# First-quad queries on a second DMA queue, last query rows moved out of the lead-in, idle transposes in their place, last token tile in two halves

## The chip, the cores and the metric

One core of a Trainium2 chip. The metric is the device time of one execution in microseconds (us). The kernels of one call ran on the same chip, with runs of the kernel before among them.

Names: TensorE is PE in the profile (PEld: its weight loads), VectorE DVE, ScalarE ACT, GpSimd POOL, SyncE SP; a trailing q (ACTq, SPq) is an engine's queue issuing transfers. The granted clock is the share of TensorE's full speed that the profile recorded; a dip is a stretch at 0.50, and a transpose is called cold when it ran at half clock. Fill is idle transposes put where TensorE would wait.

## The reference

Thresholded attention for 8 batches x 8 heads (576 rows of 64), then a gated two-matmul layer over the 4608 tokens:

```python
scores = scale * q @ k.T                       # scale = 1/8
thresh = max(scores, axis=-1) - tau
attn   = softmax(where(scores >= thresh, scores, -1e9))
x      = (attn @ v), heads side by side        # 4608 x 512
h      = x @ w_in                              # 512 x 2048
g      = h * clip(h + 3, 0, 6) / 6
out    = g @ w_out                             # 2048 x 512, float32
```

## The kernel before

The work of attention is cut into 144 slots, 9 for each quad (four heads). A slot computes scores for 128 query rows of two heads (TensorE), takes the row maximum while copying them out (VectorE), masks and exponentiates them (ScalarE) and normalizes them (GpSimd); from slot 22 on, matmuls of the gated layer fill the gaps. Before slot 0, keys and queries of the first quad must be loaded and transposed by TensorE: the lead-in. After slot 143 the rest of the gated layer runs: the tail.

```python
# loads of a quad, in this order, all on SyncE's queue: keys, queries, the last 64 rows of both, ...
def main(dst, src, h, order):
    nc.sync.dma_start(out=dst[:, :, h, :], in_=src[b, 4 * g + h, 0:512, :].rearrange(order, t=4))
...
def transpose_rest(quad):                      # last 64 rows of the four heads
    ps = bank("tr")                            # one PSUM bank
    nq, _, kr = nat[quad]
    nc.tensor.transpose(ps[:, 0:P], kr[:], identf[:])
    if by_pe(2 * quad):
        nc.tensor.transpose(ps[:, P:2 * P], nq[:, 1024:1152], identf[:])
    def evict():
        ...
        nc.vector.tensor_copy(out=qT[:, :, 512:S], in_=both[:, 1])     # query rows: used in slot 8 only
        copy_out(kT[0:64, :, S:S + 64], both[0:64, 0])                 # keys: used in slot 0
        copy_out(kT[64:P, :, 0:64], both[64:P, 0])
    return evict
...
warm_up(14)                                    # idle transposes, to raise the TensorE clock
...
evict = transpose_k(0)
warm_up(4)
evict_q = transpose_q(0)
evict()
evict_q()
transpose_rest(0)()
...
queue[0].tiles = scores(0, 0)
for n, sl in enumerate(queue):                 # the slots
    ...
    if n < 8:
        warm_up(6)
...
count = [0, 0]
def rest1(item, then):                         # tail: one gated item
    h = mm1(item, pool=ps_s if count[0] % 3 else None)     # ps_s: a pair of buffers, else a third one
    count[0] += 1
    mm1_gate(item, h, mm1_relu(h, on_act=True))
    ...
def rest2():                                   # tail: output tiles
    ...
        mm2_part(bb, mt, part, pool=ps_s if count[1] % 3 else None)
        if part == 3:
            flush()
            late.extend(mm2_out(bb, mt, on_act=(count[1] % 2 == 0)))
            count[1] += 1
```

## Time and profile before

| | kernel before |
|---|---|
| median of the first 3 runs | 561.12 us (561.0 to 562.59) |
| profiled execution | span 562.3 us, time 564.1 us, mean granted clock 0.989 |
| TensorE, ScalarE, VectorE busy | 95%, 84%, 75% |
| ScalarE's first activation (mask) of slots 0, 1, 2, 3 | 10.72, 13.59, 18.23, 21.31 us |
| last matmul to the end of the span | 558.25 to 562.3: 4.05 us |

A useful yardstick throughout is the start of each slot's first ScalarE activation (its mask). Slots follow each other in a fixed pattern, so two kernels' masks differ by a constant "lead" wherever nothing new happens; a step in the lead shows where time was won or lost. The lines themselves are shown with the prediction.

### The profile page before, as it was taken

The page shows a single profiled execution, that of the slowest core. Times are in us where ns is not written, and L with a number is a line of the kernel's source. Part 1 is how long each engine was busy: PE and PEld are TensorE (multiplying, and loading weights), DVE is VectorE, ACT ScalarE, POOL GpSimd, SP SyncE. Part 2 cuts the span into 40 slices and gives each one's busy share as a digit, 9 for nine tenths or more (in the row PEclk, how much of TensorE's full clock was granted, in tenths as well). Part 3 has the DMA queues.
Part 4 walks back from the last instruction along what each step waited for, and adds up shares of the span by engine and source line. Part 5 has one row for each costly group of instructions (what it writes and reads, how often), then busy time and mean ns, then how long its engine had stood idle before and what let it go on. Part 6 is the DMA issues. An engine that isn't in the chain of part 4 may idle for free.

```text
span 562.3 us, 11634 instructions
## 1 busy us (share of the span) xinstructions
PE 535.0 (95%) x3856; PEld 309.3 (55%) x3856; DVE 424.4 (75%) x1040; ACT 470.3 (84%) x999; POOL 305.2 (54%) x646
## 2 busy tenths in 40 slices
PE   7998798899999999999999999999999999999997
PEld 5665455455545565555555565655555565654663
DVE  3588787687878788787878798887978798883440
ACT  4799899798988999989898999899898999983540
POOL 1678878854556555655456555755556555561000
PEclk8899999899999999999999999999999999999999
DMA  5879999997689876978589867987699865453102
GB/s 110 135 110 166 162 160 184 207 148 144 112 159 153 151 153 127 208 139 155 114 150 170 159 137 146 174 160 146 127 137 175 167 124 117 101 109 86 38 20 75
DMA packets 286204, 77.52 MB, mean 138 GB/s; under 512 B 269248, under 2 KB 281536, under 8 KB 286144
## 3 DMA queue, kind: packets, MB, share of 16 engines
q1 hardware_dynamic: 268736, 67.86, 64.8%
q0 software_dynamic: 17408, 8.92, 13.7%
q8 instruction: 30, 0.49, 0.4%
q14 instruction: 30, 0.25, 0.2%
HBM read 36.70 MB, written 9.44 MB: 82 GB/s over the span
## 4 chain that ended last, share of the span: by engine, by line
PE 58%; DVE 11%; ACT 9%; issue 4%; POOL 1%; DMA 1%; SPq 1%; DVEq 0%; POOLq 0%
PE h L353 18%; PE o L382 17%; PE s L256 16%; DVE s L277 5%; ACT s L285 4%; PE av L323 3%; ACT s L290 3%; DVE g L370 2%; DVE r L364 2%; ACT r L362 2%; PE s L262 1%; PE tp L213 1%; PE ar L323 1%; DVE osb L390 1%; POOL pn L298 1%
## 5 line engine op out<-in xcount | busy, mean ns | idle before, releaser
L298 POOL TENSOR_SCALAR pn<-s,rinv 128x576 bf16<-128x576 f32 x288 | 211.6, 745 | 133.5 <-issue 58.5
L277 DVE TENSOR_SCALAR_CACHE_REDUCE s<-s 128x576 f32<-128x576 f32 x288 | 205.9, 752 | 44.9 <-PE s L256 35.2
L285 ACT ACTIVATE s<-s,bias 128x576 f32<-128x576 f32 x288 | 207.1, 766 | 36.8 <-POOL bias L280 35.7
L290 ACT ACTIVATE s<-s 128x576 f32<-128x576 f32 x288 | 192.7, 671 | 0.3
L256 PE MATMUL s<-kT,qT 64*128 64x288 f32 x1024 | 172.7, 435 | 5.4 <-DVE s L277 3.2
L353 PE MATMUL h<-xT,w_in_sb 128*128 128x320 bf16 (+1 forms) x1024 | 145.0, 287 | 5.5 <-DVE g L370 4.6
L382 PE MATMUL o<-w_out_sb,g 128*128 128x512 bf16 x576 | 140.9, 379 | 3.6 <-DVE osb L390 3.0
L353 PEld LDWEIGHTS <-w_in_sb 128*128 128x128 bf16 x1024 | 92.0, 97 | 68.4 <-issue 31.1
L256 PEld LDWEIGHTS s<-kT,qT 64*128 64x128 f32 x1024 | 94.8, 188 | 62.7 <-DVE s L277 24.9
L370 DVE SCALAR_TENSOR_TENSOR g<-r,h 128x512 bf16<-128x512 f32 (+1 forms) x128 | 96.4, 754 | 41.2 <-ACT r L362 39.3
L280 POOL TENSOR_SCALAR bias<-m 128x1 f32<-128x1 f32 x288 | 54.4, 189 | 69.0 <-DVE s L277 48.2
L382 PEld LDWEIGHTS <-g 128*128 128x128 bf16 x576 | 55.6, 98 | 58.2 <-issue 9.8
L362 ACT ACTIVATE r<-h,three 128x640 f32<-128x640 f32 (+1 forms) x74 | 54.4, 737 | 21.1 <-PE h L353 20.4
L290 ACT ACTIVATION_READ_ACCUMULATOR s<-s 128x1 f32 x288 | 54.2, 188 | 0.0
L364 DVE TENSOR_SCALAR r<-h 128x512 f32<-128x512 f32 (+1 forms) x54 | 40.5, 751 | 0.0
L390 DVE TENSOR_SCALAR osb<-o 128x512 f32<-128x512 f32 x31 | 21.0, 676 | 22.2 <-PE o L382 22.2
L323 PE MATMUL av<-pT,vm 128*64 128x512 bf16 x256 | 34.6, 392 | 2.0 <-ACT kT L203 2.0
L323 PEld LDWEIGHTS <-vm 128*64 128x64 bf16 x512 | 18.1, 111 | 25.2 <-issue 18.3
L293 DVE RECIPROCAL rinv<-rsum 128x2 f32<-128x2 f32 x144 | 23.0, 160 | 10.2 <-ACT s L290 9.5
L335 DVE CAST xT<-av 128x512 bf16<-128x512 f32 x32 | 21.8, 681 | 5.6 <-PE av L326 5.3
L277 DVE DVE_READ_ACCUMULATOR s<-s 128x1 f32 x288 | 23.9, 83 | 0.0
L388 ACT ACTIVATE osb<-o 128x512 f32<-128x512 f32 x5 | 3.0, 597 | 23.9 <-PE o L382 23.9
(42 smaller groups left out, 255.9 us busy)
## 6 DMA issues: line engine op xcount, KB each, us to landing
km<-in_k_dram SPq DMA_DIRECT2D x64, 128.0 KB, 3.0
out_dram<-osb SPq DMA_DIRECT2D x32, 256.0 KB, 2.4
nq<-in_q_dram SPq DMA_DIRECT2D x96, 72.0 KB, 2.7
vm<-in_v_dram POOLq DMA_DIRECT2D x16, 256.0 KB, 5.4
nq<-in_q_dram SPq DMA_DIRECT2D x16, 128.0 KB, 3.9
w_in_sb<-in_moe_w_in_dram POOLq DMA_DIRECT2D x16, 128.0 KB, 4.1
w_out_sb<-in_moe_w_out_dram POOLq DMA_DIRECT2D x16, 128.0 KB, 4.5
pT<-pn SPq DMA_TRANSPOSE x119, 3.4
```

Source lines behind the costliest of these rows:

```text
L256: nc.tensor.matmul(tiles[a][:, hf, 0:HALF], qT_of(pair)[a * 64:(a + 1) * 64, t * P:(t + 1) * P], keys(pair, a, hf), start=True, stop=True)
L277: nc.vector.tensor_scalar(out=sl.s[:, i, :].rearrange("p (a b) -> p a b", a=2), in0=ps[:, :, 0:HALF], scalar1=1.0, scalar2=None, op0=Alu.m ...
L280: nc.gpsimd.tensor_scalar(out=sl.bias[:, i:i + 1], in0=sl.m[:, i:i + 1], scalar1=-scale, scalar2=tau, op0=Alu.mult, op1=Alu.add)
L285: nc.scalar.activation(out=s, in_=s, func=Act.Prelu, bias=sl.bias[:, i:i + 1], scale=scale, alpha=REJECT)
L290: nc.scalar.activation(out=s, in_=s, func=Act.Exp, accum_out=sl.rsum[:, i:i + 1])
L298: nc.gpsimd.tensor_scalar(out=pn[:, i, :], in0=sl.s[:, i, :], scalar1=sl.rinv[:, i:i + 1], scalar2=1.0, op0=Alu.mult, op1=Alu.mult)
L323: nc.tensor.matmul(ps[a * 64:(a + 1) * 64, :], vm[:, 2 * hp + a, c * D:(c + 1) * D], pT[:, 5 * a + c, cols], start=(c == 0), stop=False)
L353: nc.tensor.matmul(hps[:, n, 0:w], w_in_sb[:, ki, (ni + n) * P:(ni + n + 1) * P], xT[b][:, ki, c0:c0 + w], start=(ki == 0), stop=(ki == KI ...
L362: nc.scalar.activation(out=r, in_=hps, func=Act.Relu, bias=three[:])
L364: nc.vector.tensor_scalar(out=r, in0=hps, scalar1=3.0, scalar2=0.0, op0=Alu.add, op1=Alu.max)
L370: nc.vector.scalar_tensor_tensor(out=gbuf[:, ni:ni + 2, c0:c0 + w], in0=r, scalar=6.0, in1=hps, op0=Alu.min, op1=Alu.mult)
L382: nc.tensor.matmul(o_ps[0], gbuf[:, ni, mt * P:(mt + 1) * P], w_out_sb[:, ni, :], start=(ni == 0), stop=(ni == NI - 1))
```

## The change

Four things: (1) the first queries are issued by ScalarE's queue, beside the keys on SyncE's; (2) the first quad's last query rows are transposed in slot 1; (3) six and eight idle transposes fill the places where TensorE waited; (4) in the tail the buffer rotation starts at 1, and the last token tile leaves in two halves, one by ScalarE and one by VectorE.

```diff
-        def main(dst, src, h, order):
-            nc.sync.dma_start(...)
+        def main(dst, src, h, order, by=nc.sync):
+            by.dma_start(...)
...
-                    main(..., q, 2 * n + a, "(t p) d -> p t d")
+                    main(..., q, 2 * n + a, "(t p) d -> p t d",
+                         by=nc.scalar if quad == n == 0 else nc.sync)
...
-    transpose_rest(0)()
+    transpose_rest(0, of_q=False)()
+    warm_up(6)
...
+        elif n == 1:
+            evict = transpose_rest(0, of_k=False)
...
+        if n == 0:
+            warm_up(8)
         if n + 1 < len(queue):
             queue[n + 1].tiles = scores(queue[n + 1].quad, queue[n + 1].slot)
...
-    count = [0, 0]
+    count = [1, 0]
+    def last_out():
+        ...
+        nc.scalar.activation(out=osb[:, 0:c], in_=o_ps[0][:, 0:c], func=Act.Copy, scale=1.0 / 6.0)
+        nc.scalar.dma_start(out=out[r0:r0 + P, 0:c], in_=osb[:, 0:c])
+        nc.vector.tensor_scalar_mul(out=osb[:, c:2 * c], in0=o_ps[0][:, c:2 * c], scalar1=1.0 / 6.0)
+        nc.sync.dma_start(out=out[r0:r0 + P, c:2 * c], in_=osb[:, c:2 * c])
```

More of the change, by code (lines that the diff above doesn't have):

```diff
@@ L85, in load_quad @@
         nq, km, kr = nat[quad]
-        def main(dst, src, h, order):
-            nc.sync.dma_start(out=dst[:, :, h, :], in_=src[b, 4 * g + h, 0:512, :].rearrange(order, t=4))
+        def main(dst, src, h, order, by=nc.sync):
+            by.dma_start(out=dst[:, :, h, :], in_=src[b, 4 * g + h, 0:512, :].rearrange(order, t=4))
         def blocks_q(n, a, j):
@@ L97, in load_q @@
                 for a in range(2):
-                    main(nq[:, 0:1024].rearrange("p (t h d) -> p t h d", h=4, t=4), q, 2 * n + a, "(t p) d -> p t d")
+                    main(nq[:, 0:1024].rearrange("p (t h d) -> p t h d", h=4, t=4), q, 2 * n + a, "(t p) d -> p t d",
+                         by=nc.scalar if quad == n == 0 else nc.sync)
             else:
@@ L226, in transpose_k, with transpose_rest @@
         return lambda: copy_out(kT_of(pair)[:, 64:576], ps[:])
-    def transpose_rest(quad):
+    def transpose_rest(quad, of_k=True, of_q=True):
         ps = bank("tr")
         nq, _, kr = nat[quad]
-        nc.tensor.transpose(ps[:, 0:P], kr[:], identf[:])
-        if by_pe(2 * quad):
+        of_q = of_q and by_pe(2 * quad)
+        if of_k:
+            nc.tensor.transpose(ps[:, 0:P], kr[:], identf[:])
+        if of_q:
             nc.tensor.transpose(ps[:, P:2 * P], nq[:, 1024:1152], identf[:])
@@ L237, in evict @@
             both = ps[:].rearrange("p (w n t) -> p w n t", n=2, t=64)
-            if by_pe(2 * quad):
+            if of_q:
                 nc.vector.tensor_copy(out=qT[:, :, 512:S], in_=both[:, 1])
-            copy_out(kT[0:64, :, S:S + 64], both[0:64, 0])
-            copy_out(kT[64:P, :, 0:64], both[64:P, 0])
+            if of_k:
+                copy_out(kT[0:64, :, S:S + 64], both[0:64, 0])
+                copy_out(kT[64:P, :, 0:64], both[64:P, 0])
         return evict
@@ L525 @@
     last = NQUAD - 1
-    count = [0, 0]
+    count = [1, 0]
+    def last_out():
+        osb = o_pool.tile([P, d_model], F32, tag="osb", name="osb")
+        r0, c = B * S - 64 - P, d_model // 2
+        nc.scalar.activation(out=osb[:, 0:c], in_=o_ps[0][:, 0:c], func=Act.Copy, scale=1.0 / 6.0)
+        nc.scalar.dma_start(out=out[r0:r0 + P, 0:c], in_=osb[:, 0:c])
+        nc.vector.tensor_scalar_mul(out=osb[:, c:2 * c], in0=o_ps[0][:, c:2 * c], scalar1=1.0 / 6.0)
+        nc.sync.dma_start(out=out[r0:r0 + P, c:2 * c], in_=osb[:, c:2 * c])
     def rest1(item, then):
@@ L539, in rest2 @@
                 flush()
-                late.extend(mm2_out(bb, mt, on_act=(count[1] % 2 == 0)))
+                if (bb, mt) == (B // 2 - 1, 8):
+                    last_out()
+                else:
+                    late.extend(mm2_out(bb, mt, on_act=(count[1] % 2 == 0)))
                 count[1] += 1
```

## The prediction

> **What bounds the kernel now.** I read the page first (clock row and chain), then the timeline of the first 24 us, one-microsecond windows of the clock there, and last the chain and timeline of the final 30 us, because the diff touches only the two ends. From the page:
>
> ```profile
> span 562.3 us, 11634 instructions
> PEclk8899999899999999999999999999999999999999
> PE 58%; DVE 11%; ACT 9%; issue 4%; POOL 1%; DMA 1%; SPq 1%; DVEq 0%; POOLq 0%
> ```
>
> TensorE carries most of the chain that ended last, ScalarE and VectorE most of the rest; DMA is 1%. The change leaves that middle alone. It can only move when the first softmax slot starts and how the end drains. The clock row shows its lowest digits (8) in the first two slices, which are the lead-in. The timeline of the lead-in (start, duration, engine, what, then idle time and its releaser):
>
> ```profile
> 1.37 3.06 PE L164 MATMUL warm<-identf 128*128 128x128 f32 x14 [1.37 <-POOL identf masks.py:199]
> ...
> 4.83 0.63 PE L213 MATMUL tp<-identf,km 128*128 128x128 f32 x4 [0.41 <-DMA km<-in_k_dram]
> ...
> 5.86 0.63 PE L213 MATMUL tp<-identf,nq 128*128 128x128 f32 x4
> ...
> 6.47 0.30 PE L231 MATMUL tr<-identf,kr 128*128 128x128 f32 x1
> 6.53 0.69 DVE L220 COPY qT<-tp 128x512 f32<-128x512 f32 x1 [4.95 <-PE tp L213]
> ...
> 7.59 0.30 PE L233 MATMUL tr<-identf,nq 128*128 128x128 f32 x1 [0.81 <-DMA nq<-in_q_dram]
> ...
> 7.92 0.29 DVE L239 COPY qT<-tr 128x128 f32<-128x128 f32 x1 [0.70 <-PE tr L233]
> 8.25 0.53 ACT L203 COPY kT<-tr 64x128 f32<-64x128 f32 x2 [2.16 <-DVE qT L239]
> ...
> 8.83 1.23 PE L256 MATMUL s<-kT,qT 64*128 64x288 f32 x6 [0.27 <-ACT kT L203]
> 9.64 0.76 DVE L277 TENSOR_SCALAR_CACHE_REDUCE s<-s 128x576 f32<-128x576 f32 x1 [1.42 <-PE s L256]
> ...
> 10.46 2.96 PE L256 MATMUL s<-kT,qT 64*128 64x288 f32 x8 [0.39 <-DVE s L277]
> ...
> 17.14 0.76 DVE L277 TENSOR_SCALAR_CACHE_REDUCE s<-s 128x576 f32<-128x576 f32 x1 [2.84 <-PE s L256]
> ...
> 18.23 1.45 ACT L285 ACTIVATE s<-s,bias 128x576 f32<-128x576 f32 x2 [1.59 <-POOL bias L280]
> ```
>
> The reader is to see a chain of waits: the last query rows (eighth in one queue) land at 7.6, their transpose, then the VectorE copy, then the ScalarE key copies, then the first scores at 8.83. Then the second score set takes 2.96 us, where the same eight take 1.23 to 1.24 later. The windows tell why (busy columns, then granted clock, DMA share, GB/s):
>
> ```profile
> 10.00:11.00 1.00, 0.61 (x3) 0.29 (x2) 1.00 (x4) 0.28 (x1) 0.19 (x1) 0.96 0.99 224
> 12.00:13.00 1.00, 1.00 (x4) 0.44 (x2) 0.49 (x1) 1.00 (x4) 0.35 (x1) 0.50 0.00 0
> 17.00:18.00 1.00, 1.00 (x8) 0.96 (x7) 0.86 (x3) 0.00 (x0) 0.00 (x0) 0.62 0.22 20
> ```
>
> The clock is 0.50 from about 11.0 to 17.8; the 1.59 us of ScalarE idling at 18.23 is its price. At the end:
>
> ```profile
> 540.07 0.69 DVE L370 SCALAR_TENSOR_TENSOR g<-r,h 128x512 bf16<-128x512 f32 x1 [0.18 <-ACT r L362]
> ...
> 540.81 17.43 PE L382 MATMUL o<-w_out_sb,g 128*128 128x512 bf16 x80 [0.62 <-DVE g L370]
> ...
> 558.27 0.60 ACT L388 ACTIVATE osb<-o 128x512 f32<-128x512 f32 x1 [6.31 <-PE o L382]
> ```
>
> TensorE waits 0.62 us for a gate before its last 80 matmuls, then one 0.60 us eviction and one transfer close the run.
>
> **What the Trainium skill says.** (1) "TensorE: Matmul & The Clock Gate", section "What's actually happening": the array runs at half clock by default and after idling, full after about one busy window of 3.4 us, and the window runs free of the kernel's start. The trace agrees: the dip of 11.0 to 17.8 is 6.8 us, two such windows; a second dip begins near 106.6, 28 windows of 3.413 us after 11.0. Also the first 14 idle transposes need 3.06 us (0.22 each) while four at 4.83 take 0.63, so the clock really was low until about 4.2, although the records call it full there. (2) "DMA: Bandwidth & Descriptors", section "Issuing engines are not separate DMA queues": a second issuer saves only issue time, the transfers share the same engines. Here one issue costs about 0.6 us on the SyncE queue, so that is what the two moved transfers give back. (3) "PSUM — Partial Sum Buffer", section "PSUM bank collisions raise a hardware error": two engines must not use one bank and quadrant together, reads included. The trace agrees in that ScalarE's key copies waited for VectorE's query copy out of the same bank, though they read other columns and the key transpose was done at 6.77.
>
> **The change part by part.**
>
> *First queries on ScalarE's queue.* Two issues leave SyncE's queue, so the remaining first-quad transfers go out 2 x 0.6 = 1.2 us earlier. The queries were just in time (no wait at 5.86, after four idle transposes that remain), so this alone saves nothing on TensorE. ScalarE pays 1.2 us of issuing before its table load of 1.28 us: 0.74 + 1.2 + 1.28 = 3.2, before its first copy at 5.5. Against it, keys and queries now share the engines. Between 2 and 4 us the DMA moved 126 and 150 GB/s, against 254 between 4 and 5, so there is room; I allow 0.2 us (my choice) for later keys.
>
> *Last query rows out of the lead-in.* This removes the 0.81 us wait, the transpose, and the 0.29 us copy ahead of the key copies. New order: key remainder transposed at 6.47, key copies 6.8 to 7.35; query copy done at 7.22; six idle transposes at (0.60 - 0.27)/3 = 0.11 each (four take 0.60, one alone 0.27) end their issue near 7.25. The scores then start at about 7.3 to 7.4. Before, the bulk started at 8.83, with one of the four matmuls already done (0.2 us). So the first VectorE pass starts at about 7.3 + 1.0 = 8.3 instead of 9.64: 1.3 us, less 0.2 for the later keys, is 1.1. The rows are transposed in slot 1 instead, where TensorE and VectorE (0.27 us) have room, and are needed only in slot 8.
>
> *Idle transposes.* TensorE's gaps of 0.41, 0.8, 0.7 and 0.4 us before 10.5 shrink to the first. The eight after slot 0 take 0.9 us from about 8.6 to 9.5, while the second scores could start near 9.05 (first bank read): a delay of about 0.4, hidden, since ScalarE is busy with slot 0 until about 12.2. If the clock stays full, set two takes 1.24 instead of 2.96 and set three likewise. ScalarE then runs back to back: slot masks at 9.4, 12.2 and 15.1 (1.45 + 1.34 + about 0.1 each), against 10.72, 13.59 and 18.23. Of the 3.1 us at slot 2, 1.3 is the start and about 1.7 is the clock. Because the window runs free, each execution meets it in another phase: the three timed runs spread over 561.0 to 562.59 and the profiled one took 564.1 us. I count the 1.7 at 60% (my choice): 1.0.
>
> *Rotation count starting at 1.* Twenty-one gated items close the run. Before, the last two used the pair of buffers the output tiles rotate through, and the first output tile of the tail waited for item 19's gate, ending at 540.76. Now items 18 and 19 use them, and the tile waits for item 18's gate (539.89), already done when TensorE finishes at 540.19. It saves 0.6 us.
>
> *Last tile in two halves.* Both read one bank, so by (3) I expect them one after the other. ScalarE, 256 columns: from 0.585 at 512 and 0.26 at 128, 0.85 ns a column plus 0.15, so 0.37. VectorE, from 0.69 and 0.29: 0.43. With a handover of 0.04 the second half is ready at 0.84 instead of 0.60, a loss of 0.24. Its transfer is 128 KB instead of 256 KB; the last transfer moved data from about 559.7 to 560.5, some 0.75 us, so half saves 0.37. Net 0.1.
>
> Sum: 1.1 + 1.0 + 0.6 + 0.1 = 2.8 us off 561.12, so **558.3 us**. Nearly all should survive the middle: slots 3 to 20 repeat the same pattern, and TensorE did not wait for a DMA between 10 and 80 us.
>
> **The rivals.** *The clock falls anyway*, in this phase or a little later: gaps of a like size occur near 22 us without a dip, and short-row float matmuls may count as little activity. Then 1.8 is left, 559.3. *The keys are slowed by the shared engines*: if the engines alternate evenly, the keys land up to 0.6 us later, all transposes move, and with the full clock gain lost too it is 559.9 or so. For it: one transfer of 128 KB takes about 0.5 us at the full rate. Against it: half-empty engines between 2 and 4 us. *The whole clock gain arrives in every run*, and the dip near 106.6 (which also slows a TensorE stretch on the chain) goes by shifted phase: another 0.7 to 1.7, so 556.6 to 557.6. *The gain is absorbed* by a transfer or an in-order queue in the middle: the chain shows DMA and SyncE's queue at 1% each, so at most a part.
>
> **Range and chances.** Everything at risk sums to about 4.5 us and 2% is 11.2 us, so the verdict is nearly certain; the range reflects clock phase (1.7), keys (0.5) and run spread (1.5). Predicted 558.3, range 556.2 to 560.4; faster by over 2%: 0.01, within 2%: 0.98, slower: 0.01.
>
> **What would show it.** Right if the first scores run near 7.4 and the first VectorE pass starts near 8.4; if the clock is 1.00 from 10 to 18 and the second score set takes about 1.24; if slot 2's mask starts near 15 to 15.5; if the last 80 matmuls start without a gate wait; and if the VectorE half of the last tile starts only after the ScalarE half. Wrong if the key transposes start after 5.3, if the clock still shows 0.50 in the first 20 us, if the lead over the kernel before shrinks between slot 3 and the tail, or if both halves overlap.

## The result, and the profile after

The changed kernel takes 560.28 us (median of 6 runs, 559.43 to 560.52); the kernel before 562.65 us (6 runs, 561.0 to 563.4). The ratio is 0.996, 95% interval 0.9941 to 0.9979. Ratios here are the mean time of one kernel's fast runs over that of the other's of the same rounds, so not quite the ratio of the medians. In microseconds the ratio is a gain of about 2.3; the prediction had 2.8. A repeat in later rounds (e10) gave a ratio of 0.9972, about 1.6 us.

The lead-in of the changed kernel, in order of time (start, length, engine, what, then idle time before it and its releaser):

```profile
0.74 1.36 SPq L88 DMA_DIRECT2D km<-in_k_dram  x2
0.74 0.99 ACTq L88 DMA_DIRECT2D nq<-in_q_dram  x2
...
1.76 1.28 ACT L204 ACT_TABLE_LOAD   x1 [1.76 <-issue]
...
5.06 0.63 PE L214 MATMUL tp<-identf,km 128*128 128x128 f32 x4 [0.45 <-DMA km<-in_k_dram]
...
6.40 0.30 PE L234 MATMUL tr<-identf,kr 128*128 128x128 f32 x1
...
6.74 0.53 ACT L204 COPY kT<-tr 64x128 f32<-64x128 f32 x2 [0.42 <-PE tr L234]
...
7.35 1.24 PE L260 MATMUL s<-kT,qT 64*128 64x288 f32 x8
...
8.62 0.76 DVE L281 TENSOR_SCALAR_CACHE_REDUCE s<-s 128x576 f32<-128x576 f32 x1 [1.33 <-PE s L260]
...
9.54 1.81 PE L260 MATMUL s<-kT,qT 64*128 64x288 f32 x8
9.71 1.45 ACT L289 ACTIVATE s<-s,bias 128x576 f32<-128x576 f32 x2 [2.44 <-POOL bias L284]
...
15.29 1.44 ACT L289 ACTIVATE s<-s,bias 128x576 f32<-128x576 f32 x2
```

ScalarE issues two transfers first and loads its table after, at no cost, as it has nothing to do until 5.7. The key transposes start 0.23 us later than before (5.06 against 4.83). The key copies no longer wait for a VectorE copy out of the same bank. The first scores run at 7.35 in one piece, the first VectorE pass starts at 8.62 instead of 9.64, and the second score set takes 1.81 us (with a wait for its second bank inside) instead of 2.96. No stretch of the first 20 us shows a clock below 1.00 (but see e4 on the time before the clock's first record). The masks of slots 0 to 3 are at 9.71, 12.39, 15.29 and 17.98: leads of 1.01, 1.20, 2.94 and 3.33 us over the profiled kernel before.

The lead stays at 3.28 us up to slot 17. Then one-microsecond windows (busy time of PE, PEld, DVE, ACT, POOL, then granted clock, DMA share, GB/s) show this:

```profile
59.00:60.00 1.00, 0.59 (x4) 0.32 (x4) 1.00 (x4) 1.00 (x2) 1.00 (x3) 0.67 1.27 217
60.00:61.00 1.00, 0.99 (x7) 0.63 (x9) 0.07 (x3) 0.93 (x4) 1.00 (x2) 0.50 1.28 261
61.00:62.00 1.00, 1.00 (x8) 0.41 (x6) 0.78 (x2) 0.59 (x1) 0.74 (x4) 0.50 1.46 195
```

The clock fell here instead, for one window of about 3.4 us, and the lead drops to 2.00. Later the kernel before meets its own second dip, at 106.5 to 109.9, which the changed kernel does not have: the lead grows by 0.82 to 2.82 and stays there, to the last slot. So the trace adds up without a rest: 3.28 - 1.28 + 0.82 = 2.82.

The tail:

```profile
521.65 15.72 PE L357 MATMUL h<-xT,w_in_sb 128*128 128x320 bf16 x126 [0.23 <-DVE xT L347]
...
537.20 17.43 PE L386 MATMUL o<-w_out_sb,g 128*128 128x512 bf16 x78
...
554.67 0.38 ACT L541 ACTIVATE osb<-o 128x256 f32<-128x256 f32 x1 [6.31 <-PE o L386]
555.08 0.37 ACTq L542 DMA_DIRECT2D out_dram<-osb  x1
555.08 0.42 DVE L543 TENSOR_SCALAR osb<-o 128x256 f32<-128x256 f32 x1 [3.12 <-ACT osb L541]
555.54 0.33 SPq L544 DMA_DIRECT2D out_dram<-osb  x1
```

The last output matmuls follow without the gate wait (two of the 80 are missing from the records). The previous group started 2.82 us earlier than in the kernel before (521.65 against 524.47), this one 3.61 earlier (537.20 against 540.81): the rotation gave 0.79 us. The VectorE half waits for the ScalarE half. Both read one bank and both write one tile, osb; which of the two orders them is not shown. From the first eviction to the end of the span it is 554.67 to 558.7, 4.03 us, exactly what it was (558.27 to 562.3).

### The profile page after: what moved, and what is told of

It is laid out like the page before. It is cut to its first block, busy times and chain, and to the rows that moved or that the text cites. A ratio compares the mean times of both kernels' runs of the same rounds, so it can differ in the third digit from the quotient of the medians.

```text
span 558.7 us, 11624 instructions
## 1 busy us (share of the span) xinstructions
PE 530.6 (95%) x3829; PEld 309.2 (55%) x3870; DVE 424.7 (76%) x1041; ACT 469.7 (84%) x999; POOL 305.3 (55%) x646
## 4 chain that ended last, share of the span: by engine, by line
PE 55%; DVE 11%; ACT 8%; issue 4%; SPq 3%; DMA 2%; POOL 2%; DVEq 0%; POOLq 0%
PE h L357 17%; PE o L386 16%; PE s L260 15%; DVE s L281 5%; PE av L327 3%; ACT s L289 3%; ACT s L294 3%; DMA nq<-in_q_dram 2%; DVE g L374 2%; DVE r L368 2%; ACT r L366 1%; PE s L266 1%; PE tp L214 1%; SPq L310 1%; POOL pn L302 1%
## 5 line engine op out<-in xcount | busy, mean ns | idle before, releaser
L260 PE MATMUL s<-kT,qT 64*128 64x288 f32 x1024 | 169.7, 430 | 5.1 <-DVE s L281 2.8
L386 PE MATMUL o<-w_out_sb,g 128*128 128x512 bf16 x535 | 133.5, 379 | 5.2 <-DVE osb L394 3.0
L297 DVE RECIPROCAL rinv<-rsum 128x2 f32<-128x2 f32 x144 | 23.0, 160 | 11.3 <-ACT s L294 10.5
L266 PE MATMUL s<-kT,qT 64*64 64x288 f32 x256 | 20.1, 415 | 0.7 <-DVE s L281 0.7
```

Source lines behind the costliest of these rows:

```text
L260: nc.tensor.matmul(tiles[a][:, hf, 0:HALF], qT_of(pair)[a * 64:(a + 1) * 64, t * P:(t + 1) * P], keys(pair, a, hf), start=True, stop=True)
L386: nc.tensor.matmul(o_ps[0], gbuf[:, ni, mt * P:(mt + 1) * P], w_out_sb[:, ni, :], start=(ni == 0), stop=(ni == NI - 1))
```

## The experiments

Twelve kernels, all correct. Each is a change to the changed kernel unless it says otherwise. "Slot 0's mask" and "lead" are of its one profiled execution.

**e1: the lead-in alone.** Edit:

```diff
-    count = [1, 0]
+    count = [0, 0]
-                if (bb, mt) == (B // 2 - 1, 8):
+                if False:                       # last tile in one piece
```

> The changed kernel with its tail undone (rotation count from 0, last tile in one piece). My theory (the lead-in and the tail each give their part, nothing is absorbed): the mask of slot 3 starts at 18.0 as in the changed kernel, lead over the kernel before about 3.3 us there where both clocks run as in the two traces; the last 80 matmuls wait about 0.6 us for a gate again; time about 0.8 us above the changed kernel, some 1.6 below the kernel before (ratio about 0.997). Rival (the early lead is absorbed in the middle and only the tail pays): the same time as the kernel before, and a lead below 0.5 us at the last slot.

Measured: 561.99 us, before 563.02 (ratio 0.9988, 0.9968 to 1.0007). Slot 0's mask is at 10.17, slot 3's at 18.46: a lead of 2.85, not 3.3. The gate wait is back:

```profile
537.34 17.43 PE L386 MATMUL o<-w_out_sb,g 128*128 128x512 bf16 x80 [0.63 <-DVE g L374]
```

The trace holds the theory (the lead is kept to the end, at 3.47 after the dip of before; the wait returns), the time only weakly: a gain of 0.7 us (1 - 0.9988 of 563) where 1.6 was expected, with an interval that covers both and also zero.

**e2: the tail alone** (the kernel before with the new rotation and the two halves; as an edit of the changed kernel):

```diff
-        by=nc.scalar if quad == n == 0 else nc.sync
+        by=nc.sync
-    transpose_rest(0, of_q=False)()
-    warm_up(6)
+    transpose_rest(0)()
-        elif n == 1:
-            evict = transpose_rest(0, of_k=False)
-        if n == 0:
-            warm_up(8)
```

> The kernel before with the tail of the change alone. My theory: lead-in as before, first mask at 10.7; the last 80 matmuls start without a gate wait, 0.8 us earlier against the end of the matmuls before them than in the kernel before; from the end of the matmuls to the end of the span 4.05 us as before, since the halves give nothing; time about 0.8 us less than the kernel before (ratio 0.9986). Rival (the halves cost or gain): the stretch from the last matmul to the end differs from 4.05 by more than 0.1 us.

Measured: 561.16 us against 563.02 (ratio 0.9975, 0.9953 to 0.9998; 0.9986 is inside). No gate wait. First eviction to the end of the span: 3.58 us, against 4.03 in the changed kernel, which has the identical tail. The rest after the last landing differs: from the issue of the last transfer plus its 1.7 us to the end of the span, 1.01 us here and 1.46 there. So the end of the span itself has two values about 0.45 us apart (e4 has the short one too, all other traces the long one), and a single span cannot tell what the halves did. The traces with the long end can: with the last tile in one piece the stretch is 4.00 to 4.12 us (before, e1, e5), in two halves of one bank 4.03 to 4.06 (after, e3, e6, e8 to e11). The halves gave nothing.

The more important finding was not looked for. This kernel has the lead-in of before, and its trace has no clock dip there: masks at 10.76, 13.44, 16.35, 19.05, where the profiled kernel before has 10.72, 13.59, 18.23, 21.31. Its second score set, 2.96 us long in the kernel before, and its third slot's mask:

```profile
10.49 1.91 PE L260 MATMUL s<-kT,qT 64*128 64x288 f32 x8 [0.39 <-DVE s L281]
...
16.35 1.45 ACT L289 ACTIVATE s<-s,bias 128x576 f32<-128x576 f32 x2 [0.15 <-POOL bias L284]
```

The same lead-in with and without the dip differs by 21.31 - 19.05 = 2.26 us at slot 3. The dip is a matter of the execution, not of the kernel alone.

**e3 and e11: no added idle transposes** (the same kernel twice). Edit:

```diff
     transpose_rest(0, of_q=False)()
-    warm_up(6)
-        if n == 0:
-            warm_up(8)
```

> The changed kernel without the six and the eight added idle transposes. My theory (they hold the clock): the first mask still starts at about 9.6, as the start does not need them, but the granted clock falls to 0.50 somewhere between 8 and 20 us, the second or third score set takes 1.9 us or more, and the lead at slot 3 falls from 3.3 to 1 to 1.5 us; time 1 to 2 us above the changed kernel. Rival (the shorter waits alone hold the clock): clock 1.00 up to 20 us, lead at slot 3 of 3.3 or a little more, time as the changed kernel.

> The kernel of e3 again, beside the changed kernel. Theory (without the fill the clock falls in the lead-in in part of the executions): runs in two groups, part of them at a mean clock of 0.994 or lower and 1.5 to 2 us slower; median above the changed kernel by 0.3 to 1.5 us. Rival (the fill does nothing or costs its own time): same median or lower, no more low-clock runs than the changed kernel.

Measured: 560.9 us (before 563.02; ratio 0.9969) and 561.4 us (before 561.6; ratio 0.9992). Neither trace has a dip in the first 20 us, against the first expectation (leads at slot 3 of 2.76 and 3.14). But the times spread: over the twelve runs of e3 and e11 from 559.4 to 565.12, six of them above 561.2, and the six have mean clocks of 0.990 to 0.997. The changed kernel's twelve runs (the six above and e10) lie in 559.43 to 561.19, at mean clocks of 0.994 to 0.999. So the fill does not gain in every execution; what it may do is remove slow ones. This is argued from the spread, not shown. The means (561.15 without the fill, 560.28 with it) differ by 0.9 us with a standard error of 0.5. Only profiled executions say where a dip was. The slowest run, 565.12, is 5.7 us above the fastest, and its mean clock of 0.993 is worth about 4 us of TensorE time at most (an estimate: 0.007 of 565 us), so the dip alone does not explain it. And kernels with the fill have slow runs as well: 562.5 in e1 (old tail), 563.17 in e6 (four older idle transposes less).

**e4: first queries back on SyncE's queue.** Edit: `by=nc.sync` as in e2.

> The changed kernel with the first queries back on SyncE's queue. My theory (the queue change alone saves nothing, and sharing the engines cost the keys 0.23 us): key transposes start at 4.83 as in the kernel before, query transposes near 5.86, first scores at 7.2 to 7.4, first mask within 0.2 us of 9.7, lead at slot 3 of 3.2 to 3.5, time within 0.3 us of the changed kernel. Rival (the second queue is what makes the lead-in short): queries or the key remainder make TensorE wait, first scores at 7.7 or later, lead at slot 3 below 3.0.

Measured: 560.28 us against 563.02 (ratio 0.9956), the same as the changed kernel in its own rounds (0.996). But slot 0's mask is at 10.80, a whole microsecond later than expected. Its lead-in tells why:

```profile
4.91 1.09 PE L214 MATMUL tp<-identf,km 128*128 128x128 f32 x4 [0.29 <-DMA km<-in_k_dram]
5.79 1.06 PE L165 MATMUL warm<-identf 128*128 128x128 f32 x4
...
6.64 1.02 PE L214 MATMUL tp<-identf,nq 128*128 128x128 f32 x4
...
7.50 0.27 PE L234 MATMUL tr<-identf,kr 128*128 128x128 f32 x1
...
8.45 1.24 PE L260 MATMUL s<-kT,qT 64*128 64x288 f32 x8
```

TensorE waits for neither queries nor the key remainder, and from the remainder's transpose to the scores it takes 0.95 us (7.50 to 8.45), as in the changed kernel (6.40 to 7.35). What is late are the transposes: four take 1.02 to 1.09 us instead of 0.60 to 0.63. The clock had not risen yet in this execution. `prof` prints 1.00 from the start, but the clock's first record in each packed trace, at full, stands later: at 4.10 us in the kernel before, at 7.49 here and at 9.17 in e10, where the six added idle transposes still take 1.36 us instead of 0.82. The durations change where these records stand. The traces of the two lead-ins, with that time:

| run | lead-in | clock's first record, us | four key transposes, us | first scores (old lead-in: all but the first matmul), us | slot 0's mask, us |
|---|---|---|---|---|---|
| before | before | 4.10 | 0.63 | 8.83 | 10.72 |
| e2 | before | 6.01 | 1.09 | 8.87 | 10.76 |
| e5 | before, with fill | 6.68 | 1.08 | 8.96 | 10.85 |
| after | changed | 4.73 | 0.63 | 7.35 | 9.71 |
| e11 | changed, no fill | 5.42 | 0.77 | 7.54 | 9.89 |
| e1 | changed | 5.84 | 0.91 | 7.81 | 10.17 |
| e3 | changed, no fill | 6.22 | 1.09 | 7.90 | 10.26 |
| e8 | changed | 7.12 | 1.08 | 8.33 | 10.68 |
| e4 | changed, one queue | 7.49 | 1.09 | 8.45 | 10.80 |
| e10 | changed | 9.17 | 1.09 | 9.36 | 11.71 |

The lead-in of before hides a late clock behind its wait for the last query rows: with cold key transposes or not, its scores start within 0.13 us. The changed one has no wait left, and so each slow transpose shows in full: the later the clock's rise, the later the mask, in each of its seven rows. (In e10 the remainder and the six idle transposes were cold as well; no trace shows the lead-in of before in so late a case.)

**e5: the fill alone, on the kernel before.** Edit to the kernel before:

```diff
+    warm_up(6)
     transpose_rest(0)()
+        if n == 0:
+            warm_up(8)
```

> The kernel before with the idle transposes alone: six while TensorE waits for the last query rows, eight after slot 0; queue, rows and tail as before. Theory (the fill is what keeps the clock up in the lead-in; it does not shorten the waits): scores start at 8.8 as before, first mask near 10.7 plus what a later rise of the clock costs (up to 1 us), clock 1.00 from its rise up to 20 us, slot 2's mask within 5.8 us of slot 0's (7.5 in the trace of before with the dip); its timed runs lose the slow half of the runs of before (the ones at clock 0.994 and below): median 1 us under the kernel before. Rival (the dip is chance and the fill is not what stops it): the same two groups of times as the kernel before.

Measured: 561.7 us against 561.77 (ratio 0.9997, 0.9982 to 1.0011); five runs in 561.27 to 562.34. No run is slow, but the median did not fall by 1 us: in this call only one of the eleven runs of before was above 562.5. The eight transposes cost something of their own: they stand from 10.13 to 11.2 before the second scores, which start at 11.15 instead of 10.49 (e2), and slot 2's mask comes 5.90 us after slot 0's instead of 5.59. Alone, the fill is insurance with a premium; the kernel before gains nothing at the median.

**e6: without the four older idle transposes between keys and queries.** Edit:

```diff
 evict = transpose_k(0)
-warm_up(4)
 evict_q = transpose_q(0)
```

> The changed kernel without the four older idle transposes between keys and queries, which filled a wait for the queries that the second queue has removed. Theory: the queries lie there when the keys do, so the query transposes start within 0.5 us of the key transposes at full clock (0.9 at half clock), the first scores come 0.4 us earlier after the key transposes (1.9 instead of 2.3 us; e1 to e4 show 2.6 to 3.5 where the clock rose later), time 0.4 to 0.8 us below the changed kernel. Rival (the key remainder or the clock then sets the start): TensorE waits for the key remainder, or the clock rises later, and the time is the same or worse.

Measured: 560.01 us against 561.77 (ratio 0.9973; one run of the six at 563.17). First scores 2.34 us after the key transposes (5.12 to 7.46), not 1.9: the clock rose late, and the remainder's transpose waited 0.24 us for ScalarE to empty the bank that the keys had used. No gain over the changed kernel is shown by this alone.

**e7: as e6, and the last tile in two banks.** Edit, beside that of e6 (its heart; the other output tiles are as before):

```diff
+    tiles = [ps_s.tile([P, 2, 512], F32, tag="s", name="o") for _ in range(2)]
+    for i in range(2):
+        for ni in range(NI):
+            nc.tensor.matmul(tiles[i][:, 0, 0:c], gbuf[:, ni, mt * P:(mt + 1) * P],
+                             w_out_sb[:, ni, i * c:(i + 1) * c], start=(ni == 0), stop=(ni == NI - 1))
+        # i == 0: VectorE evicts, SyncE stores;  i == 1: ScalarE evicts and stores
```

> As e6, and the last token tile computed as two halves in two banks, each half evicted by its own engine, the first while the second is computed. Theory: from the last matmul to the start of the last transfer 0.38 + 0.05 us instead of 0.38 + 0.03 + 0.42 + 0.04, so 0.45 us off the end, with 0.1 us lost to the 32 shorter matmuls: 0.3 to 0.4 us below e6 and 0.7 to 1.2 below the changed kernel. Rival (an instruction fetch or the transfers set the end whatever the eviction does): the last transfer is issued earlier, and the span after it grows by as much.

Measured: 559.86 us against 561.77 (ratio 0.9968). The end of it:

```profile
553.94 0.38 ACT L391 ACTIVATE osb<-o 128x256 f32<-128x256 f32 x1 [6.35 <-PE o L385]
554.36 0.37 ACTq L392 DMA_DIRECT2D out_dram<-osb  x1
```

The last transfer is issued 0.42 us after the last eviction starts, instead of 0.87 (554.67 to 555.54), and the span ends 3.56 us after that start; issue plus 1.7 us of transfer to the end is 1.44 us, the longer of the two values of e2. So the 0.45 us are real. In the time, e7 is 0.15 us below e6 (0.3 to 0.4 were expected); that is too little to show in six runs.

**e8: the fill kept up to slot 21.** Edit: `if n < 8:` becomes `if n < 22:` before `warm_up(6)`.

> The changed kernel with the six idle transposes a slot kept on up to slot 21 instead of slot 7, because four of the five traces with half-clock windows outside the lead-in have them between 54 and 110 us. Theory (the clock falls where TensorE has gaps in those slots): no half-clock window up to slot 21 (77 us), leads kept there, median 0.3 to 0.8 us below the changed kernel. Rival (the fill costs more than it gives, as it sits in order before the work of the next slot): slots 8 to 21 take longer by 0.1 us each or more, time 1 us or more above the changed kernel.

Measured: 562.21 us against 561.77 (ratio 1.0004). No dip up to slot 21 indeed, one at 106.1. But the lead falls from 2.31 (slot 10) to 1.31 (slot 14) and from 1.31 (slot 19) to 0.39 (slot 22). The rival holds: 1.9 us lost with no dip recorded there, so the fill, which stands in order before the next slot's work, is what is left to cost them.

**e9: the last query rows in the lead-in again**, with second queue, fill and tail. Edit:

```diff
-    transpose_rest(0, of_q=False)()
+    transpose_rest(0)()
-        elif n == 1:
-            evict = transpose_rest(0, of_k=False)
```

> The changed kernel with the last query rows transposed in the lead-in again (queue, fill and tail as changed). Theory (what shortened the start is that the rows' transfer, transpose and copy no longer stand ahead of the key copies): TensorE waits for the rows for 0.1 to 0.5 us, ScalarE's key copies wait for VectorE's row copy, and from the key remainder's transpose to the first full score set passes 1.7 to 2.0 us instead of the 0.95 of the changed kernel; first mask 0.7 to 1.0 us later at the same rise of the clock; time 0.5 to 1.0 us above the changed kernel of the same call. Rival (the earlier issue alone is enough): below 1.2 us, time as the changed kernel.

Measured: 561.27 us, with the changed kernel at 560.42 (e10); their intervals against the kernel before (0.9969 to 1.0005 and 0.9956 to 0.9989) overlap. The clock rose early here as in the first trace of the changed kernel (key transposes 0.63 us), so the two compare:

```profile
6.52 0.27 PE L236 MATMUL tr<-identf,nq 128*128 128x128 f32 x1
...
7.20 0.28 DVE L242 COPY qT<-tr 128x128 f32<-128x128 f32 x1
...
7.38 1.95 PE L260 MATMUL s<-kT,qT 64*128 64x288 f32 x8
7.51 0.53 ACT L204 COPY kT<-tr 64x128 f32<-64x128 f32 x2 [1.21 <-DVE qT L242]
8.90 0.76 DVE L281 TENSOR_SCALAR_CACHE_REDUCE s<-s 128x576 f32<-128x576 f32 x1 [1.42 <-PE s L260]
```

TensorE does not wait for the rows at all: issued 1.2 us earlier, they are there. What is left is ScalarE's wait for VectorE's row copy (1.21 us, key copies at 7.51 instead of 6.74), and that costs 0.28 us at the first VectorE pass (8.90 against 8.62) and 0.59 us at slot 3 (18.57 against 17.98). The expectation of 0.7 to 1.0 us at the first mask was too high, and so was half of the theory: the 0.81 us wait for the rows goes away by the second queue alone (e9) as well as by moving the rows alone (e4). The two parts overlap; only the copy order belongs to the rows.

**e10: the changed kernel again.**

> The changed kernel unchanged, so that e9, e11 and e12 have it on the same chip. Expected: 559.4 to 560.6 us, no half-clock window in the first 20 us, first mask 9.7 to 10.3 by when the clock rose, the gate wait before the last matmuls absent.

Measured: 560.42 us against 561.6 (ratio 0.9972, 0.9956 to 0.9989), runs from 559.99 to 561.19. The profiled execution is the slowest of them, with the latest rise of the clock: slot 0's mask at 11.71 instead of 9.7 to 10.3.

**e12: as e7, with the first keys and queries split over both queues.** Edit, beside those of e6 and e7:

```diff
-        by=nc.scalar if quad == n == 0 else nc.sync           # queries
+        by=nc.scalar if quad == n == 0 and a else nc.sync     # queries and keys: second half on ScalarE's queue
```

> As e7, and the first keys and first queries split over both queues (one half of each on either), so that both key transfers are issued at 0.75 us. Theory (the keys' landing is the first wait and the second key transfer's issue, 0.6 us later, is in it): key transposes start at 4.5 to 4.8 instead of 5.06, first mask 0.2 to 0.5 us before e7's at the same rise of the clock; time 0.5 to 1.2 us below the changed kernel of the same call. Rival (the shared engines set the landing): key transposes at 5.0 or later, time as e7.

Measured: 558.83 us against 561.6 (ratio 0.9944, 0.9928 to 0.996), with the changed kernel at 560.42 (ratio 0.9972). All six runs (558.39 to 559.19) lie below all six of e10.

```profile
4.41 1.05 PE L215 MATMUL tp<-identf,km 128*128 128x128 f32 x4
5.40 0.63 PE L215 MATMUL tp<-identf,nq 128*128 128x128 f32 x4
...
7.05 1.27 PE L261 MATMUL s<-kT,qT 64*128 64x288 f32 x8
```

The keys are there as soon as the first fourteen idle transposes end; no wait is left before them. Slot 0's mask is at 9.41 although the key transposes were cold. This is the fastest of all kernels run here, 1.6 us below the changed kernel where 0.5 to 1.2 were expected. As e7 was not in this call, what the split alone gave is not shown in the time.

## Why the prediction was right, and where its terms were off

The predicted 558.3 us was a gain of 2.8; measured are 560.28 us, near the upper edge of the range, and a gain of about 2.3 by the ratio (1.6 in e10). The six runs of the kernel before, which include the three that the prediction subtracted from, have a median 1.5 us above that of these three (562.65 against 561.12). That the sum came near is in part luck, as the terms show:

- **The queue saves nothing on TensorE; the keys come 0.2 us later.** Right: e4 without it has the same time, and the key transposes started 0.23 us later. Not foreseen was that it also removes the rows' wait (e9).
- **The start, 1.1 us.** Right in the profiled pair (1.01), too large on the mean. Slot 0's mask in the six traces with the full new lead-in or that without fill (after, e1, e3, e8, e10, e11) averages 10.40, against 10.72 and 10.76 in the two traces of the old one: 0.3 us. The step that was mis-sized is "the first VectorE pass starts at about 8.3": it took every transpose at 0.11 us, while in most traced executions part of them still run at half clock, and only the old lead-in hid that. (One reading was off too: of TensorE's gaps before 10.5, the "0.7" before 8.83 is the weight loads' gap of 0.72; the matmuls' own is 0.27.)
- **The clock, 1.7 us at 60%.** Right in that the dip is in some executions and not in others. It was mis-sized: 2.26 us where it occurs (before against e2 at slot 3). How often it occurs stays open: 11 of the 39 runs of the kernel before are above 562.9 us, and none of the twelve of the changed kernel is above 561.2. The second score set took 1.81 us, not the forecast 1.24, as it waits for its second bank; e2 needs 1.91 at full clock too. That the fill holds the clock is not shown: the spread of the twelve runs without it points that way, but neither of their traces has a dip in the lead-in, and the fill alone (e5) gained nothing.
- **The rotation, 0.6 us.** Right; it measured 0.79: the 0.62 us of waiting, and 0.17 because the output matmuls now begin (537.20) before the last gated ones end in the record (521.65 + 15.72 = 537.37; ends are modelled), which the wait prevented before.
- **The two halves, 0.1 us.** The order was right: one after the other, 0.87 us to the last issue instead of about 0.63, and a last transfer of 1.7 instead of 2.0 us. Net about 0.06 us by these sizes, nothing that a time could show, and the spans show none (e2).
- **Nearly all survives the middle.** Right for transfers and queues: none of the steps in the lead falls on one. Wrong in one way that the rivals had listed as possible, and the prediction had named it as a sign of being wrong: the lead shrank between slot 3 and the tail, because the clock can fall later instead (59 us, 1.28 us lost in the profiled run). What a dip costs differs by its place: 1.6 us at 67 us in e2, nothing at 95 us in e1.

With these sizes, 0.3 for the start and 0.8 and 0.06 for the tail make about 1.2 us. That leaves 1.1 of the 2.3 us for the clock, and 0.4 of the 1.6 in the rounds of e10. The clock term is only this remainder; no run measures it on its own.

## What to carry to other kernels

A wait at the start may hide other slowness; before counting its removal in full, ask what else runs behind it (here half-clock transposes), and look at several executions, since one trace is one draw. Two measures against the same wait (earlier issue, later use) do not add, so try each alone. When a tile is to be evicted by two engines, compute it into two banks, so that the first half leaves while the second is computed (e7: 0.45 us in the trace).

## What the Trainium skill lacked or had wrong

- "TensorE: Matmul & The Clock Gate", section "Seeing it yourself", does not say that the records can lack the state before their first event (it does warn not to trust single clock events fully). In every trace here the granted clock is printed as 1.00 from 0 us, while the first fourteen idle transposes take 3.06 to 3.25 us (0.22 each, against 0.11 later) and the first record, at full, stands at 4.10 us (kernel before) to 9.17 us (e10).
- The same page, section "What's actually happening", has the clock fall after an idle window of about 3.4 us. Here it fell with far shorter gaps: at 10.9 us in the kernel before, after gaps of at most 0.81 us, and at 59.3 us in the changed kernel, where the longest gap just ahead was 0.90 us, while one of 1.40 us (before the scores at 19.57) passed without a fall. Another section of the page does have frequent short idles bring the clock down, in another kernel; what share of a window must be busy, it does not say. The free-running window of the page fits: the falls come 2 and 30 windows of 3.413 us after the first record in the kernel before, 16 in the changed kernel, 18 in e2. That the phase decides whether the lead-in has a dip is suggested by the same lead-in with one (before) and without (e2), not tested.
- "DMA: Bandwidth & Descriptors", section "Issuing engines are not separate DMA queues", calls the issue time that a second issuer saves usually small. In a lead-in of eight transfers it is not: an issue took 0.4 to 0.8 us, beside 2.3 to 3.8 us from issue to landing for the first four transfers, and issuing both key transfers at 0.75 us, ahead of the queries (e12), brought the key transposes from between 5.03 and 5.27 us down to 4.41.
